# A fused sliding-window attention and gated FFN kernel: the value product of four head groups in one run of TensorE, placed by a count of instructions

## The chip, the cores and the metric

The kernel runs on one core of a Trainium2 chip. The metric is device time in microseconds (us) of one execution. TensorE (PE) multiplies matrices, with PEld as its weight-load side; VectorE (DVE), ScalarE (ACT) and GpSimd (POOL) do the elementwise work; SyncE (SP) and GpSimd issue the DMA transfers.

## The reference

The input x has 2,048 rows of 576 numbers in bf16. With xn the layer norm of x, the kernel computes

```python
q, k, v = split(xn @ wqkv)              # 32 heads of 18
scores  = q @ k.T * 18 ** -0.5          # masked: query i sees keys i-255 .. i
s       = concat(softmax(scores) @ v) @ wo
h       = sigmoid(xn @ w_gate) * (xn @ w_up)      # 4,608 wide
out     = x + s * silu(h @ w_down)
```

## The kernel before

The rows are worked in four chunks of 512 (`NC`, index `c`). For each chunk the program builds, in this order: layer norm (`build_ln`), the value projection (`build_v`), five groups of query and key projections (`build_qk`), eight head groups of four heads each (`build_attn`, index `hg`), the output projection (`build_wo`) and the FFN with the final sum (`build_ffn`). The FFN has a first half, gate and up projection for 36 tiles of 128 hidden columns (`gate_up`, moving operand 512 columns), and a second half, the down projection (`down`, 288 columns). Down weights `wd_sb` stay in SBUF once loaded; gate and up weights (`wgs`, `wgr`) are streamed again in every chunk through four slots.

This is a list of operations with dependencies, and not yet an order. `schedule` makes the order: a greedy list scheduler with an estimated duration for each operation, a priority, and pools of PSUM. It gives each engine its fixed sequence, and `emit` writes it out with semaphores, leaving out waits that an earlier wait of the same engine covers. So attention of one chunk is woven between FFN matmuls of this chunk or the one before, and one edit anywhere moves instructions on all engines.

PSUM is used as four units of two banks. `pool_s` (units 0 and 1) serves scores, projections and value products; `pool_f` (2, 3, 1) serves the FFN. A `Hold` takes units when its first matmul is placed and gives them back when its readers are done. SBUF buffers that are used in turn are `Ring`s: a slot is written again only when its last reader is done.

Most matmuls are made by `pair` (L122): two products side by side, each on half of the array's rows, tile size 64 x 128. For a head group, `build_attn` makes five score matmul sets (`BINS`) into PSUM; ACT writes their exponentials into a slot of `expr` (L751; `NEX = 12` slots), DVE multiplies the edges by a mask (L764). For every second head group, `build_pv` makes the value product (L801) of two head groups. There the array is split into eight tiles of 64 x 32, and for each of 12 key blocks (8 in chunk 0) eight small matmuls run side by side, 96 (64) in all. Per product and half there follow on DVE a 32 x 32 block transpose out of PSUM into `ot1` (L819), the reciprocal of the softmax sum, the scaling and a transpose back (L827), and DMAs into `oT`, one half on SP's queue, one on POOL's.

Query, key, value and output weights (`wqk`, `wv_sb`, `wo_sb` with their remainders) are loaded once in chunk 0 and stay. In chunks 1 to 3 the rows of x are loaded into a ring `xr`, normalized from there into `xnr`, and transposed by DMA into `xnT`.

Of the kernel before, what the change touches and what calls it, by code (L numbers as in the profile page):

```python
# [34 lines left out]
NQS = 4  # L35
NKX = 2
NEX = 12
OENG = ("SP", "POOL")
PV_ORDER = (0, 5, -4, -3, -2, -1, 1, 2, 3, 4, 6, 7)
TURN_NS = 265.0  # L40
BINS = (((-4, 0, 1), (1, 1, 5), (6, 6, 2)),
# [12 lines left out]
NXR = 2  # L54
# [31 lines left out]
SPACE_NS = ((1500, 1500, 1400, 1500, 2000, 1200, 2000, 1100),  # L86
            (900, 1600, 1500, 1500, 1500, 2500, 1500, 1600),
            (1700, 900, 1500, 1500, 1500, 1500, 2000, 1500),
            (1500, 1500, 2500, 1100, 1600, 1500, 900, 1100))
# [100 lines left out]
class Op:  # L190
    __slots__ = ("eng", "est", "deps", "fn", "name", "prio", "start", "end", "tok", "needs_tok",
                 "nbytes", "slack", "idx", "succs", "cidx", "odeps", "acq", "lane", "filler", "space")

    def __init__(self, eng, est, fn, name, deps, prio, nbytes, odeps, acq):
# [30 lines left out]
        self.space = 0.0  # L225
        for d in self.odeps:
            assert d.eng == eng
# [22 lines left out]
class Builder:  # L250
# [17 lines left out]
    def op(self, eng, est, fn, name="", deps=(), prio=3, nbytes=0, odeps=(), acq=None):  # L268
        o = Op(eng, est, fn, name, deps, prio, nbytes, odeps, acq)
        o.cidx = len(self.ops)  # L270
        self.ops.append(o)
        for d in o.deps:
            d.succs.append(o)
        for d in o.odeps:
            d.succs.append(o)
        return o
# [12 lines left out]
    def alloc_memory(self):  # L289
# [30 lines left out]
        self.ot1, _ = seq("ot1", [P, 1, NT], f32)  # L320
# [4 lines left out]
        self.wqk, _ = seq("wqk", [P, KB - 1, 2, D])  # L325
        self.wqkr, _ = seq("wqkr", [P, D])
        self.wq4, _ = seq("wq4", [P, KB, 2, RD])
        self.wv_sb, _ = seq("wv_sb", [P, KB - 1, D])
        self.wvr, _ = seq("wvr", [P, D // 2])
        self.wo_sb, _ = seq("wo_sb", [P, KB - 1, D])  # L330
        self.wor, _ = seq("wor", [P, D // 2])
        self.qd, _ = seq("qd", [P, NQD, 2, NT])
        self.xr, _ = seq("xr", [P, NXR, D])
# [21 lines left out]
        self.pool_f = Pool("F", [2, 3, 1], last)  # L355

    def build_graph(self):
        self.r_xr = Ring(NXR, "xr")
# [6 lines left out]
        self.r_ot1 = Ring(1, "ot1")  # L365
# [21 lines left out]
        self.x_dma = {}  # L387
        self.op_wgr = {}
        self.q_slot = {}
        self.op_sp = {}  # L390
        self.sp_grp = {}
        self.hg_grps = {}
# [3 lines left out]
        for c in range(NC):  # L396
            self.build_ln(c)
            if c == 0:
                self.build_attn_consts()
            self.build_v(c)  # L400
            made = 0
            for hg in range(NHG):
                need = min(NQK, (4 * DH * (hg + 2) - 1) // P + 1)
                while made < need:
                    self.build_qk(c, made)
                    made += 1
                self.build_attn(c, hg)
            self.build_wo(c)
            self.build_ffn(c)

    def load_x(self, c, i=0):
# [8 lines left out]
        for _ in range(2):  # L420
            s_, d_ = self.r_xr.produce()
            slots.append(s_)
            dd += d_
        assert slots[1] == slots[0] + 1
        o = self.dma(self.xr[:, slots[0]:slots[0] + 2, :],
# [3 lines left out]
        for j in range(2):  # L429
            self.x_dma[st + j] = (o, self.xr[:, slots[j], :])  # L430
# [9 lines left out]
    def build_consts(self):  # L440
# [17 lines left out]
        wq, wk, wv = (self.wqkv[:, i * D:(i + 1) * D] for i in range(3))  # L458
        self.op_wqk = [self.load_nat(self.wqk[:, :, i, :], w, "dma:wqk", ("wqk", i), 5) for i, w in enumerate((wq, wk))]
        self.op_wqk += self.load_rem(self.wqkr[:, :], (wq, wk), "dma:wqkr", ("wqkr",), 5)  # L460
        for o in self.op_wqk:
            o.slack = 2500.0
        self.op_wv = [self.load_nat(self.wv_sb[:, :, :], wv, "dma:wv", ("wv",), 6)]
        self.op_wv += self.load_rem(self.wvr[:, :], (wv[:, 0:288], wv[:, 288:D]), "dma:wvr", ("wvr",), 6)
        for o in self.op_wv:
            o.slack = 5000.0
        self.op_wqk4 = [op("DVE", 420, lambda e: e.tensor_copy(self.wq4[:, 1:KB, :, :], self.wqk[:, :, :, 512:D]), "init:wq4",
                           deps=self.op_wqk, prio=2)]
        for t in range(2):
            for i in range(2):  # L470
                self.op_wqk4.append(op("DVE", 130, lambda e, t=t, i=i: e.tensor_copy(
                    self.wq4[ROWS[t], 0, i, :], self.wqkr[ROWS[1 - i], 512:D]), f"init:wq4:{t}{i}", deps=self.op_wqk, prio=2))

    def warm(self, n, dep, before, est):
# [5 lines left out]
        for i in range(n):  # L480
            w = self.op("PE", est, f_warm, f"warm:{i}", deps=[dep], prio=4, acq=None if before else h, odeps=[before])
# [27 lines left out]
    def build_ln(self, c):  # L509
# [3 lines left out]
        for i in range(BPC):  # L513
# [24 lines left out]
            sn, dn = self.r_xn.produce()  # L538
# [17 lines left out]
            if c:  # L556
                self.r_xr.release(i % 2, ap)
# [11 lines left out]
            tr = op("PE", KB * 29.5, f_tr, f"tr:{st}", deps=[ap, dup, self.op_ident, war], prio=0, acq=h)  # L569
# [37 lines left out]
    def halves(self, h, n):  # L607
        b = h.units[0] * 1024
# [6 lines left out]
    def build_qk(self, c, gi):  # L615
# [6 lines left out]
        gc = slice(gi * P, (gi + 1) * P)  # L622

        def lhs(r, t, k):
            if gi == 4:
                return self.wq4[r, k, :, :].rearrange("p i c -> p (i c)")
            return self.wqk[r, k - 1, t, gc] if k else self.wqkr[r, gc]
# [4 lines left out]
        pj = self.two("qk", f"{c}:{gi}", n, h, lhs, rhs, [self.op_xnT[c], self.op_wqk if gi < 4 else self.op_wqk4, dq], n)  # L632
# [8 lines left out]
        for u in range(H):  # L641
# [12 lines left out]
            for w, (dst, src) in enumerate(moves):  # L654
                o = self.dma(dst, src, n_ * 2 * NT * 2 // len(moves), f"dma:sp:{c}:{u}:{w}:{gi}", ("qk", par, gi),
# [3 lines left out]
                self.sp_grp.setdefault((c, gi), []).append(o)  # L659
                self.r_qd.release(sq, o)  # L660
            self.hg_grps.setdefault((c, hg), set()).add(gi)

    def two(self, kind, tag, est_n, h, lhs, rhs, deps, n, prio=1):
        lo = None
        for hi in range(2):
            def f(eng, hi=hi):
                return turn(eng, self.halves(h, n), lhs, rhs, hi)
            lo = self.op("PE", len(BLOCKS[hi]) * mm_ns(est_n), f, f"{kind}{hi}:{tag}", deps=[lo] if hi else deps, prio=prio,
                         acq=None if hi else h)
# [7 lines left out]
    def build_v(self, c):  # L677
        op = self.op
        xs = c % 2
        for i in range(BPC):  # L680
# [5 lines left out]
            vp = self.row_proj("v", st, h, lambda r, k, cols=cols: self.xnT[r, xs, k, cols], self.wv_sb, self.wvr,  # L686
                               [self.op_xnT[c][i], self.op_wv, war])
            self.xnT_rel[c].append(vp)
            self.op_v[st] = []
# [14 lines left out]
    def build_attn(self, c, hg):  # L704
        op = self.op
        qs = self.q_slot[(c, hg)][0]
        sp = [o for gi in sorted(self.hg_grps[(c, hg)]) for o in self.sp_grp[(c, gi)]]
# [18 lines left out]
        for vi, (specs, groups) in enumerate(zip(bins, masks)):  # L726
# [3 lines left out]
            def f_sc(eng, specs=specs, h=h):  # L730
                res = None
                outs = self.halves(h, NT)
                for ks, q0, nq in specs:
# [7 lines left out]
                    deps=[sp, kxo, self.r_ex.rel[self.r_ex.uses % NEX]], prio=1, acq=h, odeps=[self.last_vis])  # L741
            self.last_vis = sc
            sc.space = float(SPACE_NS[c][hg])
# [28 lines left out]
        if hg % 2:  # L772
            self.build_pv(c, hg // 2)
        if (c, hg) == (0, 1):
            pv = self.op_pv[(c, hg)]
            self.op_wo_w = [self.load_nat(self.wo_sb[:, :, :], self.wo, "dma:wo", ("wo",), 8, [pv])]
            self.op_wo_w += self.load_rem(self.wor[:, :], (self.wo[:, 0:288], self.wo[:, 288:D]), "dma:wor", ("wor",), 8, [pv])

    def build_pv(self, c, pr):
        op = self.op  # L780
        pend, self.pend = self.pend, []
        hp = self.pool_s.hold()
# [3 lines left out]
        span = {ks: (max(ks, 0), min(ks + 5, SPC)) for ks in kss}  # L786

        def f_pv(eng):
            res = None
            outs = self.halves(hp, NT)  # L790
            for n, ks in enumerate(kss):
                q0, q1 = span[ks]
                cols = slice(q0 * SW, q1 * SW)
                for g, (hg, where, _) in enumerate(pend):
                    se = where[(ks, q0)]
                    assert all(where[(ks, q)] == se for q in range(q0, q1))
                    for t in range(2):
                        o = sub_pos(c, ks) * VSZ + (2 * hg + t) * VH
                        p0 = 32 * (2 * g + t)
                        for i in range(2):  # L800
                            res = eng.matmul(outs[i][p0:p0 + VH, cols], self.v_aug[ROWS[i], o:o + VH],  # L801
                                             self.expr[ROWS[i], se, t, cols], start=n == 0, stop=n == len(kss) - 1,
                                             tile_position=(64 * i, p0), skip_group_check=True)
            return res
        est = TURN_NS + sum(mm_ns((b - a) * SW) for a, b in span.values())
        pv = op("PE", est, f_pv, f"pv:{c}:{pr}", deps=[[m for _, _, rd in pend for m, _ in rd], vdeps], prio=1, acq=hp)
        for hg, _, rd in pend:
            self.op_pv[(c, hg)] = pv
            for se in sorted({se for _, se in rd}):
                self.r_ex.release(se, pv)  # L810
        for i in range(2):
            p1, d1 = self.r_ot1.produce()
# [5 lines left out]
            def f_t1(e, i=i, p1=p1):  # L818
                return e.transpose(self.ot1[:, p1, :], self.halves(hp, NT)[i])  # L819
            t1 = op("DVE", dve_ns(NT), f_t1, f"ot:{c}:{pr}:{i}", deps=[pv, d1], prio=1)  # L820
            hp.release(t1)
            rc = op("DVE", 255, lambda e, o1=o1: e.reciprocal(o1[:, :, DH], o1[:, :, DH]), f"rc:{c}:{pr}:{i}", deps=[t1], prio=1)
            on = op("DVE", dve_ns(NT // 32 * DH), lambda e, o1=o1, o2=o2: e.tensor_tensor(
                o2[:, :, 0:DH], o1[:, :, 0:DH], o1[:, :, DH:VH].broadcast_to([P, NT // 32, DH]), ALU.mult),
                f"on:{c}:{pr}:{i}", deps=[rc, d2, self.op_o2z], prio=1)
            self.r_ot1.release(p1, on)
# [445 lines left out]
```

## Time and profile before

| what | value |
|---|---|
| median of 3 runs | 558.5 us (558.47 to 559.21) |
| the profiled execution | 558.58 us, span of its instructions 557.2 us |
| TensorE busy | 552.6 us (99%), 8,342 matmuls |
| VectorE, ScalarE, GpSimd busy | 328.4, 274.9, 210.1 us |
| value products (L801), TensorE | 20.2 us in 16 products, 1,408 matmuls |
| DMA | 67.83 MB, mean 122 GB/s |
| granted TensorE clock | 1.00 |

The time of the profiled execution is about 1.4 us longer than the span of its instructions. A line of the timeline gives the start in us, the length in us, engine, source line, operation, output and inputs, the shape of the first, and how many were merged; in brackets, the idle time of the engine before it and what ended that. L122 is the helper `pair`, so its matmuls are told apart by their tiles: `xnT,wgs` is the FFN's first half, `wd_sb,hT` its second half, `qk,kx` scores. In a list of windows each line gives the stretch, the busy time of PE, PEld, DVE, ACT and POOL with counts, the granted clock, the mean busy share of the 16 DMA engines and GB/s. Matmuls are pipelined and their recorded lengths overlap, so their starts carry the time.

### The profile page before, as it was taken

How to read it: one execution, taken by the hardware profiler on the slowest of the kernel's cores; microseconds unless marked ns; L12 is line 12 of the kernel's file. 1: busy time of each engine (PE TensorE's matmuls, PEld its weight loads, DVE VectorE, ACT ScalarE, POOL GpSimd, SP SyncE). 2: the span in 40 equal slices, each digit the busy share in tenths (PEclk: the TensorE clock that was granted, in tenths of full speed). 3: DMA queues.
4: the chain of work that ended last, by engine and by line, in shares of the span. 5: the costliest groups of instructions: out<-in, count | busy, mean ns of one | idle time of the engine just before them, and what ended most of it. 6: DMA issues, size and time to landing. Idle time of an engine off the chain costs nothing.

```text
span 557.2 us, 19237 instructions
## 1 busy us (share of the span) xinstructions
PE 552.6 (99%) x8342; PEld 339.1 (61%) x8342; DVE 328.4 (59%) x787; ACT 274.9 (49%) x379; POOL 210.1 (38%) x360
## 2 busy tenths in 40 slices
PE   8999999999999999999999999999999999999998
PEld 7454444677755545457886555645588754444787
DVE  5477788787568667674558857357567523333111
ACT  4245654443656655645656464565656433333201
POOL 5564456566245454440667444034382200000000
DMA  7988987931125535434121264234511035542010
GB/s 222 309 244 191 230 257 218 204 61 45 51 75 155 160 107 147 142 108 96 28 63 45 70 191 125 84 113 140 168 38 38 23 105 156 171 144 75 2 44 25
DMA packets 113468, 67.83 MB, mean 122 GB/s; under 512 B 18620, under 2 KB 111516, under 8 KB 113384
## 3 DMA queue, kind: packets, MB, share of 16 engines
q1 hardware_dynamic: 105960, 60.68, 40.1%
q0 software_dynamic: 7424, 5.92, 4.0%
q8 instruction: 66, 1.08, 0.8%
q14 instruction: 18, 0.15, 0.1%
HBM read 55.15 MB, written 2.36 MB: 103 GB/s over the span
## 4 chain that ended last, share of the span: by engine, by line
PE 98%; DVE 1%; DMA 0%; issue 0%; ACT 0%
PE ps L122 95%; PE ps L801 3%; DMA x<-in_A_x_dram 0%; DVE small L525 0%; DVE small L527 0%; DVE xnr L541 0%; PE ps L599 0%; DVE xnr L545 0%; ACT thf L1059 0%; DVE small L529 0%; DVE small L531 0%; DVE thf L1061 0%; DVE xf L1064 0%
## 5 line engine op out<-in xcount | busy, mean ns | idle before, releaser
L122 PE MATMUL ps<-xnT,wgs 64*128 64x512 bf16 (+1 forms) x2400 | 282.6, 368 | 0.2
L751 ACT ACTIVATE expr<-ps 128x1024 bf16<-128x1024 f32 (+4 forms) x160 | 154.8, 969 | 77.8 <-PE ps L122 77.2
L122 PEld LDWEIGHTS ps<-xnT,wgs 64*128 64x128 bf16 x2400 | 113.8, 94 | 115.1 <-DVE hT L949 1.6
L122 PE MATMUL ps<-wd_sb,hT 64*128 64x288 bf16 (+2 forms) x2448 | 156.7, 276 | 0.0
L949 DVE SCALAR_TENSOR_TENSOR hT<-tring,ps 128x512 bf16<-128x512 bf16 x144 | 98.2, 683 | 94.8 <-ACT tring L946 93.7
L946 ACT ACTIVATE tring<-ps 128x512 bf16<-128x512 f32 x144 | 86.1, 598 | 129.8 <-PE ps L122 127.6
L122 PEld LDWEIGHTS ps<-wd_sb,hT 64*128 64x128 bf16 x2448 | 112.5, 94 | 28.4
L279 POOL DMA_DIRECT2D qk<-qd x160 | 82.2, 521 | 119.8 <-PE ps L122 109.6
L764 DVE TENSOR_TENSOR expr<-expr,mask 128x128 bf16<-128x128 bf16 (+2 forms) x240 | 63.2, 297 | 62.1 <-ACT expr L751 61.6
L715 POOL TENSOR_SCALAR kx<-kprev,small 128x256 bf16<-128x256 bf16 x64 | 61.3, 967 | 28.2 <-PE ps L122 27.4
L122 PE MATMUL ps<-qk,kx 64*128 64x320 bf16 (+1 forms) x704 | 59.4, 254 | 0.0
L279 POOL DMA_DIRECT2D oT<-o2T x72 | 36.4, 513 | 58.7 <-DVE o2T L827 49.8
L122 PE MATMUL ps<-xnT,wgr 64*128 64x512 bf16 (+1 forms) x300 | 55.9, 367 | 0.0
L122 PEld LDWEIGHTS ps<-qk,kx 64*128 64x128 bf16 x704 | 31.2, 94 | 21.6 <-ACT expr L751 0.6
L122 PE MATMUL ps<-xnT,wqk 64*128 64x512 bf16 x256 | 32.6, 376 | 0.0
L819 DVE STREAM_TRANSPOSE ot<-ps 128x512 f32<-128x512 f32 x32 | 22.4, 700 | 11.6 <-PE ps L801 11.6
L715 DVE TENSOR_SCALAR kx<-qk,small 128x512 bf16<-128x512 bf16 x64 | 22.3, 378 | 4.7 <-PE ps L122 4.1
L122 PEld LDWEIGHTS ps<-xnT,wgr 64*128 64x128 bf16 x300 | 14.9, 94 | 16.6
L827 DVE STREAM_TRANSPOSE o2T<-o 128x512 bf16<-128x512 bf16 x32 | 22.7, 711 | 1.0
L637 DVE CAST qd<-ps 128x1024 bf16<-128x1024 f32 (+1 forms) x20 | 22.1, 1110 | 1.5 <-PE ps L122 1.5
L697 ACT ACTIVATE v_aug<-ps 64x288 bf16<-64x288 f32 x32 | 13.1, 409 | 17.3 <-PE ps L122 16.8
L801 PEld LDWEIGHTS ps<-expr,v_aug 64*19 64x19 bf16 x1408 | 17.2, 87 | 6.0 <-issue 3.3
(72 smaller groups left out, 291.5 us busy)
## 6 DMA issues: line engine op xcount, KB each, us to landing
wgs<-in_B_w_gate_dram SPq DMA_DIRECT2D x72, 256.0 KB, 3.4
wgs<-in_B_w_up_dram SPq DMA_DIRECT2D x72, 256.0 KB, 3.8
wd_sb<-in_B_w_down_dram SPq DMA_DIRECT2D x9, 576.0 KB, 6.3
qk<-qd POOLq DMA_DIRECT2D x100, 36.0 KB, 2.6
wgr<-in_B_w_gate_dram SPq DMA_DIRECT2D x36, 64.0 KB, 2.2
wgr<-in_B_w_up_dram SPq DMA_DIRECT2D x36, 64.0 KB, 2.4
xf<-in_A_x_dram SPq DMA_DIRECT2D x16, 144.0 KB, 2.9
out_dram<-xf SPq DMA_DIRECT2D x15, 144.0 KB, 1.8
```

Source lines behind the costliest of these rows:

```text
L122: res = eng.matmul(outs[i], lhs(ROWS[t], i), rhs(ROWS[t], i), start=start, stop=stop, tile_position=(64 * t, 0))
L279: o = self.op(eng, DMA_ISSUE_NS[eng], lambda e: e.dma_start(dst, src), name, deps, prio, nbytes=nbytes)
L637: return eng.tensor_copy(dst, self.both(h, n))
L697: return eng.activation(dst, src, ACTF.Copy)
L715: return e.tensor_scalar(self.kx[:, sx, pos:pos + n_ // SW, t, :], src.rearrange("p (s k) -> p s k", k=SW), self.half[:, t:t + 1], None, A ...
L751: return eng.activation(self.expr[:, se, :, lo * SW:NT], self.both(h, NT)[:, :, lo * SW:NT], ACTF.Exp, scale=SM_SCALE)
L764: return eng.tensor_tensor(e_, e_, m_, ALU.mult)
L801: res = eng.matmul(outs[i][p0:p0 + VH, cols], self.v_aug[ROWS[i], o:o + VH], self.expr[ROWS[i], se, t, cols], start=n == 0, stop=n == len( ...
L819: return e.transpose(self.ot1[:, p1, :], self.halves(hp, NT)[i])
L827: t2 = op("DVE", dve_ns(NT), lambda e, p2=p2, p3=p3: e.transpose(self.o2T[:, p3, :], self.o2[:, p2, :]), f"ot2:{c}:{pr}:{i}", deps=[on, d3 ...
L946: th = op("ACT", act_ns(NT), lambda e: e.activation(self.tring[:, st, :], bank(h, 0), ACTF.Tanh, scale=0.5), f"th:{c}:{ft}", deps=[pg, dt_ ...
L949: mu = op("DVE", dve_ns(NT), lambda e: e.scalar_tensor_tensor(self.hT[:, ft, :], self.tring[:, st, :], 1.0, bank(h, 1), ALU.add, ALU.mult) ...
```

## The change

The value product is made for four head groups (`PVG = 4`) as two operations of two head groups each, which the scheduler must place one right after the other on TensorE (`then`, `nxt`). The run takes two of all four PSUM units at once from a new pool `pool_v`. `expr` grows from 12 to 20 slots, which a run's four head groups fill, and `ot1` now lives in slots of `expr`.

The scheduler counts TensorE's instructions as it goes (`at`: two for a matmul, which is a weight load and a product, and one for every second new wait), and places a run only where `fits` allows: with edges every 256 instructions (the first at 193), the 64 instructions ahead of an edge and the 256 behind it may hold at most 248 of the run.

SBUF for the longer ring comes from the weights. Query and key weights are loaded in groups of 128 columns through two slots `wqg`, for each chunk again; value and output weights share one tile `wvo` and are loaded for each chunk again. `xr` is gone, and rows of x are loaded straight into `xnr` and normalized in place. `qk` has three slots instead of four. The copies of the fifth group's weights (`wq4`) are gone. Scores are spaced by one number for each chunk instead of one for each head group. The scores of a head group wait only for the DMAs of that head group.

```diff
-NQS = 4
+NQS = 3
-NEX = 12
+NEX = 20
+NWQ = 2
+PVG = 4
+FETCH = 256
+FETCH_AT = 193
+FETCH_AHEAD = 64
+FETCH_MAX = 248
-SPACE_NS = ((1500, 1500, 1400, 1500, 2000, 1200, 2000, 1100),
...
+SPACE_NS = (2000, 2000, 2000, 1700)
...
+        self.ot1 = nc.alloc_sbuf_tensor_at("ot1", [P, NEX, NT], f32, offset=zex)
-        self.wqk, _ = seq("wqk", [P, KB - 1, 2, D])
...
+        self.wqg, _ = seq("wqg", [P, NWQ, KB - 1, 2 * P])
+        self.wqgr, _ = seq("wqgr", [P, NWQ, P])
+        self.wvo, _ = seq("wvo", [P, KB - 1, D])
+        self.wvor, _ = seq("wvor", [P, D // 2])
-        self.xr, _ = seq("xr", [P, NXR, D])
...
+        self.pool_v = Pool("V", [0, 1, 2, 3], last)
...
+    def load_wq(self, c, gi):
+        sw, dw = self.r_wq.produce()
+        wq, wk = (self.wqkv[:, i * D:(i + 1) * D] for i in range(2))
+        w = P if gi < 4 else RD
...
+        ds = [self.dma(main[:, :, i, :], both[RD:D, i, :].rearrange("(k p) c -> p k c", p=P), ...
+    def load_vo(self, c, w, name, deps):
+        ds = [self.load_nat(self.wvo[:, :, :], w, f"dma:{name}:{c}", (name,), 6, deps)]
...
-        sp = [o for gi in sorted(self.hg_grps[(c, hg)]) for o in self.sp_grp[(c, gi)]]
+        sp = self.op_sp[(c, hg)]
...
-        if hg % 2:
-            self.build_pv(c, hg // 2)
+        if hg % PVG == PVG - 1:
+            self.build_pv(c, hg // PVG)
...
-        hp = self.pool_s.hold()
+        hold = self.pool_v.hold(PVG // 2)
...
+        for n in range(PVG // 2):
+            pair2 = pend[2 * n:2 * n + 2]
...
+            pv = op("PE", est, f_pv, f"pv:{c}:{run}:{n}", deps=[] if n else deps, prio=1, acq=None if n else hold, odeps=[before],
+                    ni=16 * len(kss))
+            if before:
+                before.then = pv
+            else:
+                pv.run = 16 * len(kss) * (PVG // 2)
...
+            self.build_o(c, run * (PVG // 2) + n, hold, n, pv)
...
+    def fits(at, n):
+        ahead = (FETCH_AT - at) % FETCH
+        parts = [ahead] if n >= ahead else []
+        edge = ahead
+        while edge < n:
+            parts.append(min(n, edge + FETCH) - max(0, edge - FETCH_AHEAD))
+            edge += FETCH
+        return max(parts, default=0) <= FETCH_MAX
...
+                    if e == "PE" and nxt is not None and o is not nxt:
+                        continue
+                    if o.run and not self.fits(at + len(self.new_waits(o, known)) // 2, o.run):
+                        continue
...
+            if o.eng == "PE":
+                waits = self.new_waits(o, known)
+                known.update(waits)
+                at += o.ni + len(waits) // 2
+                nxt = o.then
```

## The prediction

> **What bounds the kernel now.** I read the page first, then the timeline around value products, the weight-load engine's idle times, and the windows of chunk 0.
>
> ```profile
> span 557.2 us, 19237 instructions
> PE 552.6 (99%) x8342; PEld 339.1 (61%) x8342; DVE 328.4 (59%) x787; ACT 274.9 (49%) x379; POOL 210.1 (38%) x360
> PE 98%; DVE 1%; DMA 0%; issue 0%; ACT 0%
> q1 hardware_dynamic: 105960, 60.68, 40.1%
> q8 instruction: 66, 1.08, 0.8%
> ```
>
> The chain that ended last is TensorE nearly throughout, at a granted clock of 1.00. So only time between matmul starts counts: an edit on another engine is worth nothing unless TensorE waits for it. The q8 row is TensorE's program: 66 packets of 16 KB for its 16,904 instructions (a matmul is a weight load and a product), so one fetch per 256.
>
> Timeline of TensorE at two value products (start, length, line, shape, count):
>
> ```profile
> 163.11 0.59 PE L122 MATMUL ps<-xnT,wgs 64*128 64x512 bf16 x4
> 163.54 0.38 PE L122 MATMUL ps<-xnT,wgr 64*128 64x512 bf16 x2
> 163.85 1.34 PE L801 MATMUL ps<-expr,v_aug 64*19 64x320 bf16 x96
> 165.13 0.40 PE L122 MATMUL ps<-qk,kx 64*128 64x64 bf16 x6
> ...
> 290.56 0.65 PE L122 MATMUL ps<-wd_sb,hT 64*128 64x288 bf16 x8
> 291.14 1.34 PE L801 MATMUL ps<-expr,v_aug 64*19 64x320 bf16 x96
> 292.42 0.39 PE L122 MATMUL ps<-qk,kx 64*128 64x64 bf16 x6
> ```
>
> Read the starts, not the lengths. Two pairs of 512 columns take 163.54 - 163.11 = 0.43 us, 0.215 a pair; the pair just ahead of the value product takes 163.85 - 163.54 = 0.31, so entering costs 0.095. The product lasts 165.13 - 163.85 = 1.28 us, the same at 291.14. Its 2,560 columns at 0.42 ns each are 1.08 us. Of the other 0.20, the starts in the trace put 0.12 behind the last group (0.178 us until the next start, where its 128 columns need 0.056); the rest is a fixed few ns per group. Over the 16 products entries are 0.092 to 0.110 us and exits 0.115 to 0.122, 3.4 us together.
>
> Weight loads, with the idle time before them:
>
> ```profile
> 22.12 0.53 PEld L122 LDWEIGHTS ps<-xnT,wgs 64*128 64x128 bf16 x6
> 23.21 0.33 PEld L122 LDWEIGHTS ps<-xnT,wgs 64*128 64x128 bf16 x6 [0.56 <-PE ps L122]
> ```
>
> Here the second half of an FFN turn waits for its own first half; the matmul starts slip 0.23 us. It happens twice (also at 45.75). Other slips after 12 us are small: 0.10 at 167.4, 0.09 at 316.5, 0.07 at 69.8.
>
> DMA in chunk 0 (window, TensorE busy, and at the right DMA share and GB/s):
>
> ```profile
> 1.00:20.00 19.00, 18.21 (x362) 13.40 (x364) 9.80 (x34) 8.02 (x14) 13.06 (x16) 1.00 0.92 270
> 20.00:40.00 20.00, 19.93 (x218) 10.20 (x216) 12.34 (x28) 6.77 (x14) 9.98 (x21) 1.00 0.96 276
> 40.00:60.00 20.00, 19.93 (x202) 9.28 (x200) 16.20 (x48) 10.95 (x17) 7.73 (x14) 1.00 0.73 176
> 60.00:80.00 20.00, 20.00 (x265) 10.01 (x262) 16.21 (x44) 11.65 (x18) 11.88 (x21) 1.00 1.04 258
> 80.00:104.00 24.00, 24.00 (x306) 11.90 (x302) 20.25 (x54) 12.17 (x19) 12.66 (x22) 1.00 0.84 228
> ```
>
> Up to 104 us the DMA engines have little left: 1.5 + 0.8 + 5.4 - 0.8 + 3.8 = 10.7 us idle. Later the share is 0.35. TensorE does not wait for them yet.
>
> **The change, part by part.**
>
> *Runs.* The built order has the same 8,342 matmuls of the same shapes, and 8 unbroken value runs instead of 16 (two of 256 instructions in chunk 0, six of 384). Between the halves of a run the tile shape does not change, so 8 entries and 8 exits go: 8 x (0.095 + 0.12) = 1.72 us, all on TensorE. If the drain came back between halves, this would be 0.
>
> *Turns that wait for themselves.* The new order has one such place, in chunk 3, instead of two: -0.23 us. The three small slips go with the order too; new ones of that size may come, so -0.3 to +0.3, taken at -0.1.
>
> *Semaphore instructions on TensorE.* 265 instead of 219. In 1,232 FFN pair-to-pair steps of the trace the 219 show 0.7 ns a step above the column pace, so 46 more cost under 0.05 us: 0.
>
> *Program fetch.* A run of 384 instructions passes in 2.4 us, and the next block must come meanwhile. In the built order the 320 instructions around the fullest fetch edge hold 249 of a run (the count in the kernel is one off), then 241 and 237 with FFN second-half work around them. At 1.16 us per 192 value instructions and 0.123 us per four FFN ones, the fullest lasts 1.5 + 2.2 = 3.7 us. In the trace, fetches in second-half stretches have landed 2.1 to 3.2 us after the start of that stretch (the packets take 0.88 to 1.41), and the shortest such stretch there, 4.7 us, shows no slip. So 0, with little left: 0.5 us. If it fails, it fails at three edges, up to about 1 us each: 0 to +3.
> [...]
>
> *Weights reloaded.* Query and key weights now come in groups, in each chunk, in rows of 256 B; value and output weights share a tile and come in each chunk. Packet records of q1 show 18 ns for 256 B (all transposes inside the chip), 27 for 512 and 51 for 1,152. A chunk needs 4,608 packets of 256 B and 1,024 of 128 (about 13 ns): 6.0 us of the 16 engines; value and output weights 3.7 us. Before, both came once, 7.4 us. So 4 x 9.7 - 7.4 = 31 us more DMA, 5.7% of the span. In chunks 1 to 3, at a share of 0.35, it is hidden. In chunk 0 it is 6.0 - 3.7 for its own groups and 2.6 for two groups of chunk 1 taken early: 4.9 us into 10.7 idle, so 0. The first 14 transfers stand as before.
> [...]
>
> *What queues behind new waits.* On SP 94 more issues at about 0.56 us are 53 us; SP now waits over 330 us in total. Value and output weights wait for the last user of the tile, with FFN weights queued behind; these have four slots of 8.6 us of first-half work, against waits of at most 28 us in the table of SP's waits. Loads of x wait for the transposes of the tile they overwrite; their users come over 10 us later. Cost 0; without that cover, one landing, 3.4 to 4.7 us, per late load.
>
> *Scores and banks.* A run holds all 20 expr slots and two of four bank pairs. Scores then wait while FFN matmuls fill TensorE; the bank pairs come free after four VectorE transposes of 0.70 us, 2.8 us, while one FFN turn in the other pairs lasts 4.3. VectorE is busy 59%. Cost 0; without cover 1.4 us a run (two more transposes than before). The last run stands 2,013 instructions before the end (3,055 before), still over 50 us, so attention is not last. Five small VectorE copies of weights go, hidden.
>
> **Sum.** 558.58 (profiled execution: span 557.2 and 1.4 around it) - 1.72 - 0.23 - 0.1 = 556.5; the median of the runs is 0.08 below that execution: 556.4 us, 0.37% faster. About 0.2% (1.1 us) is what a measurement of this kernel can tell from no change, so 557.4 to 559.6 counts as the same.
>
> **Rivals.**
>
> *A. Chunk 0 becomes DMA-bound (slower).* For it: shares of 0.92 to 1.04, and packets of 256 B from HBM that the trace never shows. Against: 10.7 us idle. If a packet takes t ns, the added work is 432 t - 2,900 ns; it fills the idle time at t = 31, and at about 25 if only half of that can be used in this order. At t = 40, 14.4 us more against 10.7 is +3.7: TensorE first waits for loads between 60 and 110 us, and the time is about 560.1; only the excess over the idle time counts. Chance 0.15.
>
> *B. The fetch takes back what the turn gave (no change).* Three edges at up to 1 us, or 1.4 us of bank waits at one or two runs: 556.4 + 1.0 to 3.0, middle 558.4. For it: 0.5 us of room. Against: no slip in any stretch of the trace. Chance 0.14.
>
> *C. The change does not do what it says*: the array drains between halves. Then only 0.33 goes: 558.2, also no change. Against: tile positions and shapes are the same in both halves, and inside a product steps between groups of that kind show 2 ns. Chance 0.02.
>
> **How the numbers follow.** The forecast has 0.69. Its own range, 555.8 to 557.2, comes from 1.7 to 1.9 for the runs (exits of the 0.115 to 0.122 kind, entries up to 0.110), -0.3 to +0.3 for slips, and 0.3 for scatter of runs. The range reaches through most of B: 555.7 to 558.8; A and the upper tail of B stay outside. Faster 0.70 (forecast and the mildest of B); same 0.15 (B, C); slower 0.15 (A).
>
> **What would show it.** In the profile after: eight L-line groups of value products of 128 or 192 matmuls each without a step inside; entries and exits as before, 8 of each; the same time per run of columns; TensorE still 99%. Right if the sum of idle and slips falls by about 2 us. B would show as a gap inside or just behind a value run with a q8 packet landing at its end. A would show as TensorE waiting for VectorE, a load or a weight tile between 40 and 110 us, with a DMA share of 1 there. I would be wrong in kind if TensorE waited for banks after a run, or for output weights ahead of the output projection.

## The result, and the profile after

The changed kernel takes 557.62 us in the median of 22 runs (556.68 to 558.31) against 558.49 for the kernel before (22 runs, 558.22 to 559.21): a ratio of 0.9982, 95% interval 0.9976 to 0.9989. That is 0.87 us less, some 40% of the 2.1 that were forecast, and below the 1.1 us that the prediction called the least that can be told from no change; the interval excludes equality, but not a gain under 0.2%. It lies inside the range, but only because the range was drawn wide enough to reach through most of rival B: the forecast's own range, 555.8 to 557.2, was missed, and by the prediction's own limits (557.4 to 559.6) the result counts as the same, an outcome that was given a chance of 0.15. Its runs scatter more than those of before, 1.6 us against 1.0.

The profiled execution took 558.17 us, 0.41 less than that of before. Its page:

```profile
span 556.8 us, 19419 instructions
PE 550.5 (99%) x8342; PEld 354.8 (64%) x8342; DVE 323.4 (58%) x782; ACT 272.4 (49%) x379; POOL 208.2 (37%) x360
PE 98%; DMA 1%; SPq 0%; issue 0%; DVE 0%; ACT 0%
q1 hardware_dynamic: 133704, 68.71, 46.8%
q8 instruction: 66, 1.08, 0.8%
```

TensorE is still the whole chain, but DMA has 1% of it where before it had 0: that is one wait of 0.53 us for up weights at 8.0 us, in the start. Busy time of PE fell by 2.1 us and the span by 0.4: the other 1.7 us are idle time that was not there before, 1.1 of them in the first 12 us. The recorded lengths hide part of each later stall, so those are read from the starts along TensorE's timeline. First a value run as it should be, then one that is broken (start, length, line, shape, count, and in brackets the idle time before it):

```profile
323.08 2.47 PE L813 MATMUL ps<-expr,v_aug 64*19 64x320 bf16 x192
325.48 0.82 PE L124 MATMUL ps<-xnT,wgs 64*128 64x512 bf16 x6
...
379.63 1.59 PE L813 MATMUL ps<-expr,v_aug 64*19 64x320 bf16 x120
381.39 1.04 PE L813 MATMUL ps<-expr,v_aug 64*19 64x128 bf16 x72 [0.17 <-issue]
382.36 0.34 PE L124 MATMUL ps<-qk,kx 64*128 64x64 bf16 x3
```

Start to start the first run lasts 2.40 us and the second 2.73, of the same columns. The second is split after 120 matmuls, 241 instructions into the run with the next weight load, where its fetch edge lies (the place where one block of 256 instructions ends and the next begins: q8 has 66 packets of 16 KB for the 16,950 instructions of TensorE). "issue" says that TensorE waited for nothing that the profile shows. At the split itself the starts show a stall of 0.37 us; the seventh run (432.37 us) loses 0.36 at the same instruction. A third stall, 0.23 us, stands 3 us behind the sixth run, exactly at the next edge.

The second new place is ahead of the first output projection:

```profile
159.48 0.38 PE L124 MATMUL ps<-xnT,wgr 64*128 64x512 bf16 x2
160.12 0.67 PE L124 MATMUL ps<-wvo,oT 64*128 64x288 bf16 x8 [0.26 <-issue]
```

160.12 - 159.48 = 0.64 us for a pair of 512 columns that takes 0.215: 0.43 lost. In the trace five semaphore instructions (they wait for counts of other engines and of transfers) stand in this gap, 0.106 us apart.

Chunk 0 has more DMA work than before and, from 20 us on, no wait of TensorE (DMA share and GB/s at the right; before: 0.92, 0.96, 0.73, 1.04, 0.84):

```profile
1.00:20.00 19.00, 17.10 (x360) 12.49 (x362) 9.79 (x34) 7.91 (x14) 12.94 (x18) 1.00 0.86 226
20.00:40.00 20.00, 20.00 (x218) 10.42 (x214) 10.99 (x21) 6.18 (x13) 7.96 (x17) 1.00 1.01 274
40.00:60.00 20.00, 20.00 (x208) 9.65 (x205) 13.92 (x41) 12.83 (x20) 6.02 (x11) 1.00 1.11 253
60.00:80.00 20.00, 20.00 (x205) 9.52 (x202) 13.85 (x39) 11.40 (x18) 10.18 (x17) 1.00 1.01 251
80.00:104.00 24.00, 24.00 (x399) 16.60 (x397) 18.59 (x48) 10.67 (x17) 9.61 (x16) 1.00 0.96 232
```

TensorE is busy throughout from 20 us on; the idle 1.9 us of the first row lie in the start, where before had 0.8 (the start varies between executions, see below).

### The profile page after: what moved, and what is told of

Its sections match the earlier page's. It is cut to its first block, busy times and chain, and to the rows that moved or that the text cites. A ratio compares the mean times of both kernels' runs of the same rounds, so it can differ in the third digit from the quotient of the medians.

```text
span 556.8 us, 19419 instructions
## 1 busy us (share of the span) xinstructions
PE 550.5 (99%) x8342; PEld 354.8 (64%) x8342; DVE 323.4 (58%) x782; ACT 272.4 (49%) x379; POOL 208.2 (37%) x360
## 4 chain that ended last, share of the span: by engine, by line
PE 98%; DMA 1%; SPq 0%; issue 0%; DVE 0%; ACT 0%
PE ps L124 95%; PE ps L813 3%; DMA wgs<-in_B_w_up_dram 1%; SPq L286 0%; ACT thf L1083 0%; PE ps L609 0%; DVE thf L1085 0%; DVE xf L1088 0%
## 5 line engine op out<-in xcount | busy, mean ns | idle before, releaser
L124 PE MATMUL ps<-xnT,wgs 64*128 64x512 bf16 (+1 forms) x2400 | 284.7, 368 | 0.6 <-DMA wgs<-in_B_w_up_dram 0.5
L124 PEld LDWEIGHTS ps<-xnT,wgs 64*128 64x128 bf16 x2400 | 117.1, 94 | 109.4 <-issue 1.2
L124 PE MATMUL ps<-wd_sb,hT 64*128 64x288 bf16 (+2 forms) x2448 | 156.2, 276 | 0.1
L124 PEld LDWEIGHTS ps<-wd_sb,hT 64*128 64x128 bf16 x2448 | 122.8, 94 | 19.7 <-issue 0.4
L776 DVE TENSOR_TENSOR expr<-expr,mask 128x128 bf16<-128x128 bf16 (+2 forms) x240 | 64.4, 295 | 69.4 <-ACT expr L763 68.4
L124 PE MATMUL ps<-qk,kx 64*128 64x320 bf16 (+1 forms) x704 | 62.0, 254 | 0.0
L124 PE MATMUL ps<-xnT,wgr 64*128 64x512 bf16 (+1 forms) x300 | 56.6, 367 | 0.0
L124 PEld LDWEIGHTS ps<-qk,kx 64*128 64x128 bf16 x704 | 34.5, 94 | 24.8 <-ACT expr L763 1.3
L124 PE MATMUL ps<-xnT,wqg 64*128 64x512 bf16 (+1 forms) x320 | 38.2, 355 | 0.0
L124 PEld LDWEIGHTS ps<-xnT,wgr 64*128 64x128 bf16 x300 | 15.4, 94 | 16.0
L841 DVE STREAM_TRANSPOSE ot<-ps 128x512 f32<-128x512 f32 x32 | 20.3, 688 | 7.7 <-PE ps L813 7.7
L124 PEld LDWEIGHTS ps<-xnT,wqg 64*128 64x128 bf16 x320 | 16.5, 94 | 10.9 <-issue 0.3
L1085 DVE TENSOR_TENSOR thf<-thf,s_attn 128x576 bf16<-128x576 bf16 (+2 forms) x5 | 2.0, 399 | 34.3 <-ACT thf L1083 34.3
```

Of the source, the lines that this page charges most:

```text
L124: res = eng.matmul(outs[i], lhs(ROWS[t], i), rhs(ROWS[t], i), start=start, stop=stop, tile_position=(64 * t, 0))
L776: return eng.tensor_tensor(e_, e_, m_, ALU.mult)
L841: return e.transpose(self.ot1[:, p1, :], self.halves(hp, NT, un)[i])
L1085: q2 = op("DVE", dve_ns(w, 2.0), lambda e: e.tensor_tensor(t, t, s_, ALU.mult), f"fq2:{nm}", deps=[th, self.op_s[sb]], prio=0)
```

## The experiments

Theory F: the stalls at 241 are TensorE waiting for its own program; a block of 256 instructions is fetched only about one block ahead. Rivals are named in the expectations. Ratios are to the kernel before on the same chip, whose median was 558.48 to 558.90 us there.

**The changed kernel again (e1, e11).**

> The changed kernel itself, once more, for a second profile and a time beside its variants. Theory F (program fetch): both value runs that stand 241 instructions ahead of a fetch edge stall again, 0.36 us each, and the step behind the first of them again loses 0.23; 0.96 us in all, since nothing in this depends on chance. Theory T (the stalls are late transfers that happened to collide in one execution): stalls of another size or at other places. Time expected 557.6 +- 0.4 by both.

> The changed kernel once more, as the measure for e10 on the same chip: a ratio to the kernel before of 0.998, a wait of 0.4 to 0.65 us ahead of the first output projection, no gap at the third run, and 0.4 to 1.0 us in the stalls at the two runs 241 instructions ahead of an edge and behind the first of them.

Measured: 557.41 us, ratio 0.9982 (0.9973 to 0.9991), and 558.28, 0.9989 (0.998 to 0.9998). The stalls come back at the same instructions, but not with the same length. Ahead of the two edges: 0.37 and 0.36 us in the first profile, 0.09 and 0.35 in e1, 0.44 and none in e11; behind the sixth run 0.23, none and 0.50. So "nothing in this depends on chance" was wrong, and the place is right. The wait ahead of the output projection was 0.43, 0.65 and 0.47. The first 12 us cost 3.91, 3.51 and 3.92 us above the pace of the columns (the time between matmul starts beyond what their columns need), 3.76 before the change: no more than the scatter of single executions.

**Runs ending on an edge (e4).**

```diff
-FETCH_MAX = 248
+FETCH_MIN = 241
...
-        return max(parts, default=0) <= FETCH_MAX
+        return ahead >= FETCH_MIN
```

> Every run must start with 241 or more of its instructions ahead of the fetch edge; the built order has 242, 243, 252, 247, 249, 241, 254 and 252. Theory F: eight stalls, 0.36 us at 241 and 0.025 to 0.05 us more for each further instruction (what an instruction of a gate or down product takes beyond one of a value product): 0.36, 0.4, 0.4, 0.6, 0.65, 0.75, 0.75 and 0.8, together about 4.7 us, and up to 0.25 behind each run that is followed by half-size products: 560.5 to 563. Theory T: 557.6 +- 0.5, with no gap at instruction 241 to 254 of the runs.

561.52 us, ratio 1.0046 (1.003 to 1.0061), as theory F says; the other theory is out. That the sum came out at the expected 4.7 is luck: eight stalls of at most 0.8 us were expected, and four of the eight runs stall, 0.7 to 1.6 us each, while four (those 241, 243, 247 and 249 ahead) do not. The worst:

```profile
214.92 1.63 PE L813 MATMUL ps<-expr,v_aug 64*19 64x320 bf16 x126
217.95 0.27 PE L813 MATMUL ps<-expr,v_aug 64*19 64x128 bf16 x8 [1.40 <-issue]
```

126 matmuls are 252 instructions, and its edge is 252 ahead.

**No placement (e3).**

```diff
-FETCH_MAX = 248
+FETCH_MAX = 10000
```

> The limit on the placement is taken away; the built order has two runs with a whole block of 256 instructions between two fetch edges inside the run (107 and 5 ahead of the first edge), and none at 241. Theory F: the block that follows is asked for at the edge inside the run, its packet begins about 2.0 us after such an edge in the changed kernel's trace, takes 0.9 to 1.4 and is usable 1.5 later, while the whole block runs in 1.6 us: a stall of 1 to 3.5 us at each of the two, so 558.6 to 563.5. Theory T: no loss at these places, 557.6 +- 0.4.

565.39 us, 1.0127 (1.0113 to 1.0141): above the range. The two runs with a whole block inside lose 1.67 and 2.49 us, as expected; four more places lose 0.4 to 1.0 each that were thought safe. And the largest one costs a second time (timeline, then windows with the granted clock in the third column from the right):

```profile
367.54 1.71 PE L813 MATMUL ps<-expr,v_aug 64*19 64x320 bf16 x130
371.53 1.62 PE L813 MATMUL ps<-expr,v_aug 64*19 64x192 bf16 x62 [2.28 <-issue]
```

```profile
369.00:372.00 3.00, 0.72 (x54) 0.56 (x41) 1.29 (x2) 0.00 (x0) 1.28 (x2) 0.95 0.25 70
372.00:375.00 3.00, 3.00 (x58) 1.66 (x44) 1.31 (x2) 0.00 (x0) 0.00 (x0) 0.50 0.02 5
```

Behind 2.28 us of idle time TensorE ran at half its clock for about 3 us, 1.5 us more.

**At most 234 on either side (e2), at most 200 (e5).**

```diff
-FETCH_MAX = 248
+FETCH_MAX = 234
...
-        return max(parts, default=0) <= FETCH_MAX
+        return ahead <= FETCH_MAX and n - ahead <= FETCH_MAX
```

(200 in place of 234 in e5.)

> A run may start only where at most 234 of its instructions lie ahead of the first fetch edge and at most 234 behind it; the built order has 77, 29, 233, 199, 233, 152, 195 and 215 ahead. Theory F: no stall within or just behind a run; 0.96 us less than the changed kernel, less or plus 0.3 for the order, which differs from the sixth run on: 556.3 to 557.0 against 557.6. Theory T: the same time as the changed kernel within 0.3 us, with stalls of 0.2 to 0.4 us elsewhere. In both the step ahead of the output projection of chunk 0 (0.43 us) stays, since the order up to there is the same but for the second run.

> A run may start only where at most 200 of its instructions lie ahead of the first fetch edge and at most 200 behind it, so that no block of 256 holds more than 200 of a run: 77, 189, 197, 184, 197, 194, 195 and 197 ahead. Theory F2: what counts is time, not instructions: TensorE's sequencer runs up to 42 instructions ahead of the array, the packet of the next block starts about 1.4 us after it passes an edge, takes 0.9 to 1.4, and the block is used 1.3 to 1.6 us after that, so the array needs work for about 4 us from 42 instructions ahead of an edge to the next edge. With 56 or more other instructions in each block that holds nearly everywhere: at most 0.1 us at one or two edges, 0.5 to 1.0 less than the changed kernel: 556.4 to 557.0. Theory P (the order pays elsewhere what it gains here): 557.2 to 557.8, with new waits of TensorE. The wait ahead of the first output projection, 0.43 and 0.65 us in the two profiles of the changed kernel, stays in both.

Both missed. e2: 558.45 us, 1.0003 (0.9994 to 1.0012), 1 us slower than the changed kernel instead of 1 us faster. e5: 560.09, 1.0027 (1.0015 to 1.0038). In e2 the runs at 241 are gone, but it stalls by 0.84 us behind a run with 227 instructions after its edge, by 0.61 in a run 233 ahead that passes freely in the changed kernel, and by 0.39 behind one with 232 after the edge. In e5 no run stalls inside, but the block behind one that has 190 instructions after its edge, followed by half-size down products, stalls by 1.33 us:

```profile
386.05 0.25 PE L124 MATMUL ps<-qk,kx 64*128 64x192 bf16 x2
387.46 0.31 PE L124 MATMUL ps<-qk,kx 64*128 64x320 bf16 x2 [1.16 <-issue]
```

One more edge (93.1 us) loses 0.25. Four steps that are at no edge lose 0.30 to 0.35 each, one of them a turn that waits for its own first half. So the number of a run's instructions in a block is not what decides. In e5 an edge inside a run, with little work behind it, cost 1.33 us, within the 0.7 to 1.6 of the stalls in e4.

**Two runs moved by 32 (e9), with e8 as its measure.**

```diff
                 # e8
-                o.slack = 1000.0
+                o.slack = 3000.0
                 # e9, besides
-FETCH_MAX = 248
+FETCH_MAX = 249
...
+        if n > ahead > 238 or (n == 384 and ahead < 0):
+            return False
```

(`ahead` is a remainder and never below 0, so the second condition never holds.)

> The changed kernel with one number altered: the planner takes the transfers of attention outputs as landing 2 us later. The built order is that of the changed kernel but for the output projections (the first one 74 instructions later); the runs stand 77, 237, 233, 199, 233, 241, 243 and 234 instructions ahead of an edge (241, 241 and 232 before in the last three). Theory L (the wait ahead of the first output projection is for the last of these transfers): it goes, 0.43 to 0.65 us less than the changed kernel: a ratio to the kernel before of 0.9970 to 0.9976, 556.8 to 557.1 where that one stands at 558.5. Theory S (six semaphore instructions in a row cost about 0.5 us wherever they stand): the wait stays and the ratio is 0.998. The fetch stalls stay by both: 0.1 to 0.4 us at 241, 0.35 to 0.45 at 243, up to 0.25 behind the first of them.

> As e8, with two runs moved by 32 instructions, from 241 and 243 ahead of the edge to 209 and 210. Theory F3: the block behind an edge that lies inside a run is asked for last, its packet begins 1.9 to 2.2 us after that edge, takes 0.9 to 1.1 and is used 1.4 to 1.5 later, 4.4 us in all. The stalls ahead of the two edges go (0.45 to 0.85 us), but the block behind the first of them then holds 174 run instructions and half-size products, about 3.5 us of work, and stalls 0.6 to 1.2; the one behind the second holds 4.2 us of work, 0 to 0.3. Net against e8: 0.2 less to 0.8 more, about 0.3 more. Theory F1 (only the instructions ahead of an edge count): 0.45 to 0.85 us less than e8.

e8: 559.05 us, 1.0008 (0.9999 to 1.0017); e9: 558.82, 1.0003 (0.9994 to 1.0012). In e9 the stalls at the two moved edges are gone and one of 0.95 us has come at the block behind the first, as theory F3 said:

```profile
386.03 0.29 PE L124 MATMUL ps<-wd_sb,hT 64*128 64x288 bf16 x2
387.10 1.15 PE L124 MATMUL ps<-wd_sb,hT 64*128 64x288 bf16 x16 [0.79 <-issue]
```

F1, which counts only what lies ahead of an edge, has no place for this stall. The times do not tell the two apart: they differ by 0.23 us, less than the intervals. Two more runs of e9 that were not moved stall at their edges, the third by 0.87 and the eighth by 0.54. In e8 the wait ahead of the output projection is gone (theory L), yet the kernel is slower than the changed one, and than the 556.8 to 557.1 that were expected: the run 243 ahead stalls by 1.61 us where 0.45 was expected at most, and another edge takes 0.53.

```profile
431.85 1.59 PE L813 MATMUL ps<-expr,v_aug 64*19 64x320 bf16 x121
434.86 1.03 PE L813 MATMUL ps<-expr,v_aug 64*19 64x128 bf16 x71 [1.42 <-issue]
```

**The output projection later, in chunk 0 alone (e10), beside e11 on the same chip.**

```diff
-                o.slack = 1000.0
+                o.slack = 3000.0 if c == 0 else 1000.0
```

> The later landing is taken for chunk 0 alone, so that from 5,450 instructions on the built order is the changed kernel's instruction for instruction, runs at the same places; only the first output projection stands 74 instructions later, and around the edge ahead of the third run (233 instructions ahead of the next one) a turn's wait for its own first half comes 1 instruction behind the edge instead of 15 ahead of it. Theory L: 0.43 to 0.65 us less ahead of the output projection. Theory W (a wait of TensorE's sequencer at an edge decides when the next block is asked for): at the next edge, inside the third run, 0.6 to 0.9 us are lost where the packet begins after that wait, as in e2 and e9, and nothing where it began before, as in e8. L alone: 0.4 to 0.65 less than the changed kernel. L with W: between 0.65 less and 0.45 more, with more scatter than the changed kernel.

558.32 us, 0.999 (0.9981 to 0.9998), against 0.9989 for the changed kernel: no difference. The profile shows what both theories expect. No wait is left ahead of the projection (0.47 in e11), and the third run, untouched but for the wait 1 instruction behind its edge, is broken at instruction 233:

```profile
200.96 1.56 PE L813 MATMUL ps<-expr,v_aug 64*19 64x320 bf16 x116
203.01 1.05 PE L813 MATMUL ps<-expr,v_aug 64*19 64x64 bf16 x76 [0.49 <-issue]
```

0.68 us in the starts. In the changed kernel the same run passes unbroken (x192, 2.47 us). The packet began 1.45 us after that wait had ended; in e2, e3 and e9, which have the wait at the same place, 1.38, 1.52 and 1.60 after it, with stalls of 0.61, 1.00 and 0.87. In e8, with the wait there too, it began 1.5 us before the wait ended, and the run passed. So one order can go either way. The profiled execution took 557.10 us, 0.98 less than that of e11 and 1.2 below the median of its own runs; that the two effects cancel in the median is therefore argued and not shown.

**The same order, four instructions later (e12).**

```diff
+                if o is shift_at:
+                    for _ in range(SHIFT):
+                        eng.wait_ge(semof(("E", "ACT")), known[("E", "ACT")])
```

(`SHIFT` is 8; eight waits make four instructions.)

> The changed kernel with four instructions more on TensorE, waits on a count that ScalarE has reached long before, put into a stretch of full-width gate products ahead of the sixth run. The order of the matmuls is the same from the first to the last; only the places against the fetch edges change, from there on by 4: the sixth and seventh run stand 237 instead of 241 ahead of an edge, the eighth 228 instead of 232. The four waits pass while the array works and cost nothing. Theory F3: the stalls at the two edges, 0.09 to 0.44 and 0 to 0.36 us in the profiles of the changed kernel, shrink by 0.1 to 0.2 each (4 instructions at 0.025 to 0.05), mostly to nothing; the one behind the sixth run (0 to 0.5) grows by up to 0.1; the first wait ahead of the output projection stays. 0.1 to 0.4 less than the changed kernel, a ratio to the kernel before of 0.9975 to 0.9985. Theory T (the stalls have to do with the transfers of that time, not with the place): the same stalls as before, a ratio of 0.9982 to 0.9989.

558.14 us, 0.9985 (0.9976 to 0.9994). In its profile the three stalls of the changed kernel have shrunk to 0.09 us together, from 0.96, 0.43 and 0.94, with the order of the matmuls unchanged. That speaks for place and against traffic, as far as one profile can, since these stalls vary from one execution to the next. The time does not show it; the interval contains the ratios of the changed kernel and most of what theory F3 expected. In this profile the output projection waits longest of all, and here the trace names the cause (timeline, then TensorE's waits):

```profile
159.60 0.38 PE L125 MATMUL ps<-xnT,wgr 64*128 64x512 bf16 x2
160.58 0.67 PE L125 MATMUL ps<-wvo,oT 64*128 64x288 bf16 x8 [0.59 <-DMA oT<-o2T]
```

```profile
PE ps L125 <- DMA oT<-o2T: 0.6, 1, 0.6
```

**Later projections with even runs (e6).** The slack of e8 on e5.

> As e5, and the planner takes the transfers of attention outputs as landing 2 us later, so that the output projections stand later in the order (the first one 117 instructions later). Theory L: the wait ahead of the first output projection is for the last of these transfers, which lands 4 us after its issue while the DMA engines are full, and the five semaphore instructions of 0.106 us behind it then pass one by one; with the projection later all of it goes: 0.4 to 0.65 us less than e5: 555.9 to 556.5. Theory S (the six semaphore instructions cost their 0.5 us wherever they stand): as e5 within 0.15 us.

560.58 us, 1.0035 (1.0021 to 1.0048), 4 us above what theory L expected. It tells nothing apart: e5 had no wait ahead of that projection either, since its order puts it 34 instructions later than the changed kernel's. It does say that six semaphore instructions in a row cost nothing there, against theory S. The stall of 1.33 at the block behind the sixth run is there again, 1.36.

**Runs of two head groups (e7).**

```diff
-PVG = 4
+PVG = 2
```

> Only the merging is undone: a run holds two head groups, 16 runs of 128 or 192 instructions with an entry and an exit each, as before the change; the reloaded weights, the larger ring and the banks stay. Leaves nothing out of the computation. Theory M (the merging is worth its 1.72 us and the reloads and the layout cost nothing): the kernel before within 0.4 us, 558.1 to 558.9, with 16 entries of 0.09 to 0.11 and 16 exits of 0.115 to 0.122, no fetch stall, and a wait of up to 0.65 ahead of the first output projection. Theory R (the reloads cost something that the changed kernel hides behind its gain): 559.3 or more, with TensorE waiting for weights or for transfers that share the DMA engines.

559.74 us, 1.0023 (1.0012 to 1.0034). 16 entries and 16 exits are back. The kernel is 1 us slower than before the change: out of theory M, and a time of theory R. Its profile, of a slower execution (560.98 us), has two waits of TensorE that neither kernel has, 1.0 us for a masked tile of a value run and 0.8 for query rows (`PE ps L124 <- DMA qk<-qd`), and 0.5 at a fetch edge. The planner's spacing of scores was set for four groups; whether these waits come from it or from the reloads, as theory R has it, was not tried apart. So this run does not show what the merging alone is worth: the changed kernel is 1.9 to 2.3 us faster than this one (1.0023 - 0.9989 and 1.0023 - 0.9982), waits included.

## Why the prediction was right or wrong

All sums here are starts above the pace of the columns, from 12 us on: 4.56 us before; 3.99, 3.70 and 3.98 in the three profiles of the changed kernel. They fell by 0.6 to 0.9, where a fall of about 2 was named as the sign of being right; the sign named for rival B, a gap at a value run with a packet of q8 landing ahead of its end, came instead.

*Runs.* Right. Entries and exits were 3.55 us in sum and are 1.82, 1.83 and 1.81: -1.73, forecast -1.72. Rival C is out; between the halves no step stands out.

*Turns that wait for themselves.* Right: one instead of two, 0.23 us, at 497 us.

*Program fetch.* This is the step that failed: "So 0, with little left: 0.5 us". It took the packet's landing for the moment at which the block can run. In the fourteen profiles no block was entered earlier than 1.1 us after the end of its packet, and all 32 gaps of over 0.26 us at an edge (up to 2.5) ended 1.1 to 1.6 us after it, whatever their length. With those 1.1 to 1.6 us the 0.5 us of room is gone. The landings of 2.1 to 3.2 us after a stretch's start, which the step used, were also the wrong sample: in the three profiles of the changed kernel the packet begins 0.8 to 2.5 us after an edge that lies in a run, and from 0.7 us before to 0.5 after one that lies ahead of it, in other work. The sequencer had run up to 42 instructions ahead of the array (the semaphore instructions show it): over 1 us of down products, 0.25 us of a run. What it costs: 0.96, 0.43 and 0.94 us.
The packet that each of these 32 gaps waited for was the one that began around the edge before it, so in these profiles only about one block of 256 lay ahead.

*What queues behind new waits.* The second failure, 0.43 to 0.65 us at "Cost 0". The step looked at output weights; the transfers that came late are the attention outputs. The second run of chunk 0 ends later than before; the last of its eighteen transfers is issued at 154.7 us, five us ahead of the projection, while the DMA engines are full (q1 alone has 90% of them from 156 to 159.6 us, with x, gate and up weights and no reloaded weight issued there), and transfers to that tile from 152 us on landed up to 4.9 us after their issue against 2.6 in the median. 154.7 + 4.9 is 159.6 us, and the first of the five semaphore instructions passes at 159.59. Before the change the distance was no longer, issue at 136.7 and projection at 141.6 us, but the transfers landed after 1.6 to 1.7 us. e8 and e10, with the projection about 3 us later, have no wait there.

*Semaphore instructions.* 0 is right where the sequencer is ahead (e5, e8, e10: six in a row, no step), and wrong behind a wait that ends late: the five that follow it pass one by one at 0.106 us. At 424 us a late wait with two of them costs 0.20 ahead of a query projection. One wait ahead of scores at 305 us costs 0.15.

*Small slips.* The 0.29 of before went with the order, as forecast 0.1 net; the new ones are the 0.20 and 0.15 above.

*Weights reloaded.* Cost 0 is right, size wrong: q1's share rose by 6.7 points of the span and not 5.7, and chunk 0 has 102.0 us of DMA share times time against 92.2, 9.7 more and not 4.9. Rows of 256 B from HBM took 18 ns a packet in the median, the value that was assumed and below the 31 at which rival A begins. TensorE waits for no reloaded weight in the profiles of the changed kernel; whether the reloads cost something in another order, as e7 may have it, is open.

*The sum.* With the means of three profiles: -1.73 - 0.23 - 0.29 + 0.78 (fetch) + 0.51 (output projection) + 0.21 + 0.15 = -0.6; the three profiled executions are 0.41, 1.11 and 0.50 below that of before. The median of 22 runs is -0.87. What is missing from the forecast is rival B below its price of 1.0 to 3.0, 0.4 to 1.0 us at three edges, plus a late landing that no rival had.

*What stays open.* When a block is asked for is not in the trace. Its packet began 1.4 to 1.6 us after a wait of the sequencer right behind an edge, in four profiles of five; in the fifth it came earlier. Why one order goes either way, which would explain the wider scatter of the changed kernel, was not settled. No version run here beats the changed kernel by more than the intervals.

## What to carry to other kernels

In a value run 384 instructions passed in 2.40 us, and the program itself became a transfer with a deadline: its packets took 0.88 to 1.45 us in the profile after, and no block was entered earlier than 1.1 us after its packet's end in the fourteen profiles. Reckon the time of work between two fetch edges, from the packet's end plus what passes until its first use, and look at the block behind a dense stretch as closely as at the one ahead of it. A count of instructions does not replace that time, and every change of order moves the edges: e2, e5 and e8 each cured one wait and paid it back, or more, at an edge elsewhere. A gain of 1.7 us that comes as reckoned is still only half visible if two transfers with small margins stand behind it.

## What was not expected of the hardware

- A stall of 2.28 us idle was followed by about 3 us at a granted clock of 0.50 (e3), 1.5 us more. Stalls of 0.5 to 1.5 us of idle time (e3, e4, e8) left the clock at 1.00.
- At the 32 gaps a block of program was used 1.1 to 1.6 us after its 16 KB packet had ended.
- Semaphore instructions on TensorE passed 0.106 us apart behind a wait that ended late; where the sequencer was ahead of the array (up to 42 instructions), six in a row left no step (e5, e8, e10).
